# Attention, soft experts and a feed-forward in one kernel: other step order, alternating transposes, four feed-forward blocks, late weight parts, rows spread by DMA

## The chip, the cores and the metric

The kernel runs on one core of one Trainium2 chip. A core has TensorE (PE, with the weight loads PEld beside it), VectorE (DVE), ScalarE (ACT), GpSimd (POOL) and SyncE (SP), which here only issues transfers, and 16 DMA engines. The metric is the device time in microseconds.

## The reference

Three layers follow each other. All inputs are float32 but for the feed-forward's two weights, which the kernel reads as pairs of 32-bit words.

```python
# 1. attention: q, k, v are (4, 8, 576, 64)
q_d, k_d, v_d = means over groups of 4 positions          # 144 positions
out_up    = repeat(softmax(q_d k_d^T / 8) v_d, 4 times)
out_local = softmax(q k^T / 8 where |i - j| < 4) v
x = (out_up + out_local) as (2304, 512)
# 2. soft experts: phi (512, 32), w1 (8, 512, 1024), w2 (8, 1024, 512)
logits = x phi
slot_in = softmax(logits over tokens)^T x                  # 32 slots, 4 for each expert
slot_out[e] = relu(slot_in[e] w1[e]) w2[e]
y = softmax(logits over slots) slot_out                    # (2304, 512)
# 3. feed-forward: w_in (512, 2048), w_out (2048, 512)
out = relu(y w_in) ** 2 w_out
```

## The kernel before

**Attention.** A unit is two heads of one batch: 16 units, four for each batch. The work of a unit is cut into some thirty pieces, each with a letter, and a step `s` runs one piece of each letter for the unit `s - LAG[letter]`, in the order of a string (`ORDER`, or `ORDERS[s]` for single steps). 19 steps are issued in this order exactly: every engine's queue gets its instructions in program order and works through them in order. The letters that matter here:

- `Q`, `L`: SP loads q and k two units ahead, and v. `l`, `o`: SP loads weights, as many as `LOADN` and `LOADO` say for the step.
- `K`, `T` (`transposes`): PE transposes k or q, head by head, ACT (and DVE for one part of four) copies the result from PSUM. PSUM's general buffers `t` are three in turn.
- `d`, `b` (`downsample`): POOL sums q or k over groups of four.
- `M`, `S`: mask and local scores on PE. `R`: maximum and difference on DVE. `E`: exponential on ACT. `n`: sums on DVE. `P`: POOL multiplies. `p`: PE transposes the probabilities, DVE copies them.
- `s`, `m`, `e`, `N`, `q`: the same for the down-sampled attention (scores, maxima, three exponentials, sums and POOL's product pn, transposes).
- `V`, `v`, `w`, `D`: the value matmuls, their sums, and the down-sampled values; ACT writes xd. `A`: DVE adds both into xt.
- `t`: logits of xt; after the last unit of a batch also the gating statistics (`stage_g1`). `X`, `Y`: xt transposed into token rows. `g`, `G` (`stage_g2`, `stage_g3`): transposes and the matmul sip that gathers the slots' inputs, once for each batch.
- `F`, `H`, `J`: matmuls without use, as many as `FN` says, to keep PE at work. `c`: narrowing steps, as `CONV` says.

**Weights.** Every weight comes in pieces of 512 KB (w1 32, w2 32, w_in 16, w_out 16) in the fixed order of the list `loads`; `LPOS` says where w_in's pieces stand in it. `load_next` issues the next piece if a buffer is free: 32 of the ring, four of the pool `wa`, two and six more when attention's buffers are given up. w_in and w_out have to be narrowed from pairs of words to one float32: five operations a piece (`narrow`), on DVE, the first on ACT after the experts. `NORDER` is the order of narrowing, and `NEXP`, `NSTEPS` and `ACHAIN` say how many of these operations are issued at each place.

**Experts.** For each of eight: `expert_up` (the slots times w1, PE), `expert_mid`, `expert_down` (w2).

**Feed-forward.** As y is a product of the gates and 32 slots, `slots_in(j)` multiplies the slots by a quarter j of w_in (tile ap, 32 matmuls) and `slots_rows(j)` spreads the result over the partitions by four matmuls with a selection matrix (tile arp); ACT and DVE write the parts into `ast`. `ffn_up(c, f)` makes a 128 x 384 piece of the hidden layer from `ast` and the gates, ACT and DVE square it and split it into ghi and glo (for the pairs in `BYV` DVE takes the square for glo), and `ffn_down(c, f)` multiplies both by the split piece f of w_out: nine matmuls of 512 columns. Steps (c, f) run over six token blocks c and 16 pieces f, in blocks of f that `FB` gives; `ffn_up` is two steps ahead. At the end of a block, `partial` copies the sums out of PSUM (first block) or adds them to what is kept (DVE, later blocks). `SPLIT` says at which step a piece of w_out is split, `SLOTS` at which step `slots_in` (i) and `slots_rows` (r) of a quarter stand; quarter 0 and quarter 1's `slots_in` are in `ACHAIN`, the list of work between the experts and the first step.

Of the kernel before, what the change touches and what calls it, by code (L numbers as in the profile page):

```python
# [22 lines left out]
NE = 8  # L23
# [15 lines left out]
CONV = {19: 3}  # L39
# [4 lines left out]
LOADN = {0: 3, 1: 2, 2: 2, 3: 2, 4: 0, 5: 1, 6: 3, 7: 3, 8: 2, 9: 3, 10: 2, 11: 4, 12: 4, 13: 4, 14: 3, 15: 3, 16: 4, 17: 3, 18: 3, 19: 3}  # L44
LOADO = {0: 1, 1: 2, 2: 1, 3: 1, 4: 1, 5: 1, 6: 1, 7: 0, 8: 0, 9: 0, 10: 2, 11: 1, 12: 2, 13: 0, 14: 0, 15: 4, 16: 2, 17: 4, 18: 3, 19: 4}
# [3 lines left out]
ORDERS = {0: 'dSqvNRKsogPleMTnHXDFAcYwEmLtbpGJQV', 1: 'dYqSREVHvnocsJLPlKwmgFAeNTDtbpGMXQ', 2: 'dYSVHREvqnlwgPKcsmGoDAeTbMNptJLQFX', 3: 'dYHSVRvEqnwlgPGKsmDFAeTNJLtpMXcoQb', 15: 'dYSVHREvqnlwgPKcsmoGDeTANtbpJLQXFM', 16: 'dYSqREVHvwngPlKoGsmDFAceJLNtbpMXQT', 17: 'dYsqVHvJLGTwgRPNloMSDFAEncetbpmXQK', 18: 'dYSVHREvqnlgPwKcmGoDAseTNtbpJLQFXM'}  # L49
FN = {'F': [0, 3, 1, 0, 0, 0, 0, 0, 0, 0, 0, 0, 0, 0, 0, 4, 1, 10, 0, 0], 'H': [6, 1, 0, 0, 0, 0, 0, 0, 0, 0, 0, 0, 0, 0, 0, 1, 0, 2, 0, 0], 'J': [1, 4, 1, 0, 0, 0, 0, 0, 0, 0, 0, 0, 0, 0, 0, 0, 9, 0, 1, 0]}  # L50
LATE = 16
LOADS = 'Q0 L0 phi Q1 L1'
START = 22
DDVE = ()
DCOPY = ((1, 0, 1),)
PCOPY = (0, 4, 5)
CHAIN = (5, 0, 4)
# [7 lines left out]
NEXP = {(3, 0): 1, (3, 1): 1, (3, 2): 1, (3, 3): 1, (4, 0): 1, (4, 1): 1, (4, 2): 1, (4, 3): 1, (5, 0): 1, (5, 1): 1, (5, 2): 1, (5, 3): 1, (6, 0): 1, (6, 1): 1, (6, 2): 1, (6, 3): 1}  # L65
WRES = 0
ACHAIN = 'S1 T f1 g2 g3 g4 n4 f2 a0 f2 r0 r1 a1 W0 n2 n1 u0 u1 f3 n1 f3'
NSTEPS = (3, 1, 2, 2, 2, 2, 2, 2, 2, 3, 1, 2, 2, 1, 0, 2, 1, 2, 2, 2, 2, 2, 1, 0, 1, 0, 1, 0, 3, 1, 1, 0, 1, 2, 0, 1, 1, 1, 2, 0, 0, 3, 1, 0, 0, 2, 1, 0, 1, 0, 1, 1, 0, 2, 1, 0, 0, 1, 3, 1, 0, 0, 1, 3)
NSTEP = 1
FB = (0, 8, 12, 16)  # L70
SPLIT = {2: 1, 4: 2, 6: 3, 8: 4, 10: 5, 12: 6, 14: 7, 26: 8, 28: 9, 36: 10, 41: 11, 50: 12, 58: 13, 65: 14, 73: 15}
# [1092 lines left out]
```

## Time and profile before

| | |
|---|---|
| time, median of 3 | 455.02 us (454.85 to 456.29) |
| profiled execution | 454.35 us, span 452.7 us |
| mean granted clock of PE | 0.97 |
| PE busy | 415.7 us, 92% of the span |
| DVE, ACT, POOL busy | 293.1, 270.3, 96.5 us |
| bytes moved by DMA | 70.54 MB |

The span runs from the first to the last instruction; the time holds the start and end of the execution too. PE's busy time counts matmuls from start to end, so it also holds matmuls that are pipelined. Attention lies before about 165 us of the profile, the experts from 173 to 218 us, and the feed-forward behind them.

### The profile page before, as it was taken

Reading aid. Unit: us, or ns where it says so; the run is one execution under the profiler, and the core shown is the slowest. Engines: PE = TensorE matmul, PEld = TensorE weight load, DVE = VectorE, ACT = ScalarE, POOL = GpSimd, SP = SyncE. Lnnn points to the kernel's source line nnn. Section 1 sums busy time; section 2 is a strip of 40 time slices with the busy share of each in tenths; the row PEclk is TensorE's granted clock in tenths of the full one; section 3 lists DMA queues with packets and bytes.
Section 4 is the critical chain, followed back from the end, with each engine's and each line's share of the span. In section 5 each row is a group of like instructions: output and inputs, shape, how many; then the busy total and the mean of one; then the engine's idle time right before and its main releaser. Section 6 shows DMA issues by size and latency. Waiting matters only on the chain.

```text
span 452.7 us, 11645 instructions
## 1 busy us (share of the span) xinstructions
PE 415.7 (92%) x4548; PEld 319.2 (71%) x4548; DVE 293.1 (65%) x693; ACT 270.3 (60%) x670; POOL 96.5 (21%) x178
## 2 busy tenths in 40 slices
PE   7898899889988879987979999999999999999996
PEld 5576667657757745542568888888888888888885
DVE  3466647765775541398599899877935646576564
ACT  3478657866766521213388987688757656544551
POOL 8555645546654500030000000000000000000000
PEclk8899989998998998996999999999999999999999
DMA  7999999999331382999998000000000000012113
GB/s 180 373 327 277 265 301 270 267 265 252 99 98 24 107 276 103 363 409 409 409 408 319 1 0 1 1 2 0 0 1 0 1 1 2 0 38 103 70 71 139
DMA packets 43248, 70.54 MB, mean 156 GB/s; under 512 B 24378, under 2 KB 24634, under 8 KB 43194
## 3 DMA queue, kind: packets, MB, share of 16 engines
q1 hardware_dynamic: 43050, 69.68, 47.1%
q8 instruction: 36, 0.59, 0.5%
q14 instruction: 18, 0.15, 0.1%
q10 hardware_dynamic: 144, 0.13, 0.1%
HBM read 65.07 MB, written 4.72 MB: 154 GB/s over the span
## 4 chain that ended last, share of the span: by engine, by line
PE 73%; DVE 9%; ACT 9%; DMA 4%; issue 2%; POOL 1%; ACTq 0%; DVEq 0%; POOLq 0%; SPq 0%
PE po L1095 43%; DMA w<-in_moe_w_dram 4%; PE up L1015 4%; PE s L446 3%; PE hp L877 3%; DVE xt L588 2%; PE so L906 2%; PE ptp L519 2%; PE xp L623 2%; ACT kz L411 2%; PE lgt L604 1%; DVE elp L458 1%; PE av L562 1%; DVE mx L457 1%; ACT xd L580 1%
## 5 line engine op out<-in xcount | busy, mean ns | idle before, releaser
L1095 PE MATMUL po<-wparts,ghi 128*128 128x512 f32 x576 | 148.4, 392 | 1.8 <-ACT ghi L1023 1.3
L1095 PEld LDWEIGHTS po<-wparts,ghi 128*128 128x128 f32 x576 | 106.9, 188 | 22.7 <-ACT ghi L1023 1.5
L1095 PE MATMUL po<-wparts,glo 128*128 128x512 f32 x288 | 81.5, 390 | 0.5 <-DVE glo L1028 0.5
L1020 ACT ACTIVATE r<-up 128x384 f32<-128x384 f32 x96 | 47.2, 492 | 55.0 <-PE up L1015 46.1
L1028 DVE TENSOR_TENSOR glo<-r,ghi 128x384 fp32r<-128x384 f32 x94 | 52.4, 557 | 35.6 <-ACT ghi L1027 31.5
L1095 PEld LDWEIGHTS po<-wparts,glo 128*128 128x128 f32 x288 | 54.0, 188 | 12.1 <-DVE glo L1028 0.9
L1024 DVE TENSOR_TENSOR r<-r 128x384 f32<-128x384 f32 x44 | 24.4, 555 | 22.2 <-ACT ghi L1023 22.1
L1015 PE MATMUL up<-cst,ast 128*128 128x384 f32 x96 | 32.9, 344 | 0.0
L500 POOL TENSOR_TENSOR pl<-elp,sm 64x350 f32<-64x350 f32 x32 | 24.7, 772 | 26.5 <-PE tr L406 20.7
L415 ACT ACTIVATE qt<-tr 64x320 f32<-64x320 f32 x64 | 28.0, 438 | 1.1
L1026 ACT ACTIVATE r<-r 128x384 f32<-128x384 f32 x50 | 26.2, 525 | 1.6
L1027 ACT CAST ghi<-r 128x384 fp32r<-128x384 f32 x50 | 25.7, 514 | 1.6
L1023 ACT ACTIVATE ghi<-r 128x384 fp32r<-128x384 f32 x46 | 24.1, 525 | 1.5
L463 ACT ACTIVATE elp<-elp 128x350 f32<-128x350 f32 x16 | 7.9, 495 | 27.2 <-DVE elp L458 27.2
L411 ACT COPY kz<-tr 64x320 f32<-64x320 f32 (+1 forms) x48 | 20.6, 429 | 3.0 <-PE tr L406 1.3
L509 POOL TENSOR_TENSOR pn<-pd,sm 128x435 f32<-128x435 f32 x16 | 14.7, 917 | 33.0 <-DVE sm L508 33.0
L428 POOL TENSOR_TENSOR s<-kz 64x288 f32<-64x288 f32 x32 | 21.2, 663 | 1.3
L1015 PEld LDWEIGHTS up<-cst,ast 128*128 128x128 f32 x96 | 18.0, 188 | 4.1 <-issue 0.6
L877 PE MATMUL hp<-w,sT 128*32 128x256 f32 x256 | 18.3, 418 | 2.4 <-DMA w<-in_moe_w_dram 1.9
L457 DVE TENSOR_REDUCE mx<-s 128x10 f32<-128x350 f32 x16 | 8.3, 518 | 18.4 <-PE s L446 18.4
L906 PE MATMUL so<-w,ht 128*32 128x256 f32 x256 | 17.6, 406 | 1.2 <-DMA w<-in_moe_w_dram 0.5
L562 PE MATMUL av<-pt,vw 64*64 64x73 f32 x640 | 14.9, 234 | 3.5 <-DVE pt L520 3.5
(205 smaller groups left out, 710.4 us busy)
## 6 DMA issues: line engine op xcount, KB each, us to landing
w<-in_moe_w_dram SPq DMA_DIRECT2D x64, 512.0 KB, 8.2
win<-in_moe_w_in_dram SPq DMA_DIRECT2D x16, 512.0 KB, 10.1
wout<-in_moe_w_out_dram SPq DMA_DIRECT2D x16, 512.0 KB, 10.9
vw<-in_v_dram SPq DMA_DIRECT2D x62, 80.0 KB, 6.2
q<-in_q_dram SPq DMA_DIRECT2D x16, 288.0 KB, 4.4
k<-in_k_dram SPq DMA_DIRECT2D x16, 288.0 KB, 4.5
out_dram<-o SPq DMA_DIRECT2D x17, 256.0 KB, 2.1
vw<-in_v_dram SPq DMA_DIRECT2D x2, 64.0 KB, 2.5
```

Of the source, the lines that this page charges most:

```text
L411: (nc.vector.tensor_copy if (j, h, r) in DCOPY else nc.scalar.copy)(out=o, in_=i_)
L415: nc.scalar.mul(out=o, in_=i_, mul=1.0 / 128.0)
L500: nc.gpsimd.tensor_tensor(out=pl[r, :, c0:c0 + W], in0=el[r], in1=sm[r, 0:NB].unsqueeze(2).to_broadcast([64, NB, W]), op=ALU.mult,)
L877: nc.tensor.matmul(t[32 * g:32 * g + 32], sT[:, kt], got["w1", e, kt][:, 256 * g:256 * g + 256], start=(kt == 0), stop=(kt == 3), tile_pos ...
L906: nc.tensor.matmul(so[32 * g:32 * g + 32], ht[:, g // 2, j], got["w2", e, j][:, g // 2, 256 * (g % 2):256 * (g % 2) + 256], start=(e == 0 ...
L1015: nc.tensor.matmul(t, ast[:, 128 * f:128 * f + 128], cst[:, c * n:c * n + n], start=True, stop=True)
L1020: nc.scalar.activation(out=r, in_=t, func=AF.Relu)
L1024: nc.vector.tensor_tensor(out=g, in0=r, in1=r, op=ALU.mult)
L1026: nc.scalar.activation(out=g, in_=r, func=AF.Square)
L1027: nc.scalar.copy(out=ghi, in_=g)
L1028: nc.vector.tensor_tensor(out=glo, in0=g, in1=ghi, op=ALU.subtract)
L1095: nc.tensor.matmul(po[c][i], a[:, 128 * i:128 * i + 128], w[f], start=(first and w is whi and a is ghi), stop=(last and a is glo), skip_gr ...
```

## The change

- **Start.** An exponential of two numbers is ACT's first instruction. The local mask is made ahead of the other constants. DVE clears kz instead of POOL. `START`, the matmuls without use ahead of step 0, goes from 22 to 24.
- **Transposes.** The five transposes of each of two heads alternate, in two PSUM buffers, instead of one head after the other.
- **Order of a step.** `ORDER` and eight `ORDERS` are new, with `LOADN`, `LOADO`, `CONV`, `FN` and `CHAIN`. In the common step, `p` now stands ahead of `t`, `M` and `b` ahead of `N` and `X`, `P` behind `D`, `d` behind `n`, `g` behind `S` and `G` ahead of `K`.
- **Loads.** w_in's first quarter stands at place 43 of `loads`; the other three come behind all experts, between w_out's pieces (`TAIL`), all into the ring. They are issued only while more than 2 + `parts` ring buffers are free, and the rest of the list goes on in the feed-forward, after each step. `parts` starts at 9, the buffers that `partial` will need.
- **Narrowing.** `NORDER`, `NEXP`, `NSTEPS`, `SPLIT` and `BYV` are new; in the experts eight narrowing calls instead of 16, all in experts 5 and 6.
- **Feed-forward.** Four blocks of four f instead of 8, 4 and 4. Quarters 1 to 3 of w_in have their `slots_in` at steps 16, 40 and 60. Behind it SP issues 16 transfers of 32 rows that spread the result into `selq` (`slots_copies`), and at steps 18, 44 and 70 `slots_split` writes `ast` from there. `slots_rows` is left for quarter 0 alone.

```diff
-ORDER = 'HYdSVREvqnlwgPKcsmoGDeTAFNtbpLJXQM'
+ORDER = 'YFSgREVLvqwndGKHJsmDPeTAoptQMbNXcl'
-CONV = {19: 3}
+CONV = {10: 1, 12: 1, 15: 3, 18: 1, 19: 2}
-FN = {'F': [0, 3, 1, 0, ..., 4, 1, 10, 0, 0], 'H': [6, 1, 0, ...], 'J': [1, 4, 1, 0, ..., 0, 9, 0, 1, 0]}
+FN = {'F': [0, 1, 1, 0, ..., 4, 0, 10, 0, 0], 'H': [10, 5, 2, ...], 'J': [1, 4, 3, 0, ..., 0, 7, 3, 0, 0]}
-START = 22
+START = 24
-CHAIN = (5, 0, 4)
+CHAIN = (5, 4, 4)
-LPOS = [30, 30, 30, 30, 42, 42, 42, 42, 72, 72, 72, 72, 76, 76, 76, 76]
-SLOTS = {2: ['r1'], 29: ['i2'], 33: ['r2'], 62: ['i3'], 64: ['r3']}
-NORDER = 'w,w w,w w,w w,w o0 o1 o2 o3 o4 o5 o6 o7 w,w o8 o9 w,w o10,o11 w,w w,w o12,o13 o14,o15'
-ACHAIN = 'S1 T f1 g2 g3 g4 n4 f2 a0 f2 r0 r1 a1 W0 n2 n1 u0 u1 f3 n1 f3'
-FB = (0, 8, 12, 16)
+LPOS = [43, 43, 43, 43]
+TAIL = 'o0 o1 i1 o2 o3 o4 o5 o6 o7 i2 o8 o9 o10 o11 i3 o12 o13 o14 o15'
+SLOTS = {16: ['i1'], 18: ['r1'], 40: ['i2'], 44: ['r2'], 60: ['i3'], 70: ['r3']}
+NORDER = 'w,w w,w o0 o1 o2 o3 w,w o4 w,w o5 o6 o7 o8 w o9 w,w o10 w o11 o12 w,w o13,w w o14 o15'
+ACHAIN = 'S1 T n1 f1 g4 g2 g3 a0 f2 n4 f1 r0 r1 W0 f2 n2 n1 f2 u0 f3 n1 u1 f3'
+FB = (0, 4, 8, 12, 16)
...
+    first = cp.tile([1, 2], F32, name="first")
+    nc.scalar.activation(out=first, in_=ones2, func=AF.Exp)
...
-            if any(j > 1 and (j, i // 2) not in win for k, i, j in got if k == "win") and kind != "win":
-                if sum(x[0] is ring for x in free) < 2:
-                    fits = [x for x in fits if x[0] is not ring]
+            if kind == "wout" or kind == "win" and j > 0:
+                if sum(x[0] is ring for x in free) <= 2 + parts[0]:
+                    return
...
-            nc.gpsimd.memset(t, 0.0)
+            nc.vector.memset(t, 0.0)
             kzs.append(t)
...
-                for h in range(2):
-                    t = bt([128, 5, 64], f"tr{u}_{j}{h}")
-                    hr = slice(64 * h, 64 * h + 64)
-                    for i in range(5):
-                        m = min(128, 9 * D - 128 * i)
-                        nc.tensor.transpose(t[0:m, i], st[nm][hr, 128 * i:128 * i + m], ident[hr, hr])
+                ts = [bt([128, 5, 64], f"tr{u}_{j}{h}") for h in range(2)]
+                for i in range(5):
+                    m = min(128, 9 * D - 128 * i)
+                    for h, t in enumerate(ts):
+                        hr = slice(64 * h, 64 * h + 64)
+                        nc.tensor.transpose(t[0:m, i], st[nm][hr, 128 * i:128 * i + m], ident[hr, hr])
...
+    def slots_copies(j):
+        raws[j] = selq
+        for g in range(4):
+            for x in range(4):
+                nc.sync.dma_start(out=raws[j][32 * x:32 * x + 32, g], in_=asb[j][32 * g:32 * g + 32])
+    def slots_split(j):
+        t = raws.pop(j).rearrange("p g c -> p (g c)")
+        a = ast[:, 512 * j:512 * j + 512]
+        nc.scalar.copy(out=a, in_=t)
+        nc.vector.tensor_tensor(out=a[64:128], in0=t[64:128], in1=a[64:128], op=ALU.subtract)
...
                 slots_in(j, up(f"ap{j}", [128, 128]))
+                slots_copies(j)
             else:
-                slots_rows(j, up(f"arp{j}", [128, 512]), range(4))
+                slots_split(j)
...
         ffn_down(*steps[i - LOOK])
+        load_next(len(loads))
```

## Rows read from the trace of the kernel before

**Rows 1.** Busy us by stretch: PE, PEld, DVE, ACT, POOL; clock, DMA share, GB/s.
```profile
102.00:104.00 2.00, 2.00 (x31) 1.48 (x33) 0.74 (x2) 1.01 (x3) 1.78 (x4) 0.50 0.89 263
200.00:210.00 10.00, 6.91 (x91) 2.80 (x91) 9.43 (x25) 3.16 (x14) 0.94 (x1) 0.84 1.03 408
237.40:291.00 53.60, 53.60 (x251) 44.49 (x254) 48.77 (x97) 44.75 (x88) 0.00 (x0) 1.00 0.18 70
291.00:345.00 54.00, 54.00 (x274) 45.19 (x263) 37.39 (x72) 40.59 (x80) 0.00 (x0) 1.00 0.00 1
```

**Rows 2.** Timeline, a plain attention step; start, us, engine, line, operation.
```profile
80.63 0.47 PE L604 MATMUL lgt<-xt,phis 128*32 128x128 f32 x16 [0.85 <-DVE xt L588]
...
80.68 1.83 ACT L415 ACTIVATE qt<-tr 64x320 f32<-64x320 f32 x4
...
82.56 0.64 PEld L446 LDWEIGHTS s<-kz,qt 128*29 128x29 f32 x40 [0.32 <-ACT qt L415]
```

**Rows 3.** Timeline, the step after a fourth unit.
```profile
90.66 0.82 PE L446 MATMUL s<-kz,qt 128*29 128x70 f32 x40
...
99.08 0.41 ACT L580 ACTIVATE xd<-av 128x288 f32<-128x288 f32 x1 [2.34 <-PE av L575]
...
103.37 1.24 PE L446 MATMUL s<-kz,qt 128*29 128x70 f32 x40
```

**Rows 4.** Chain that ended last, experts; start, us, what.
```profile
191.40 1.86 PE so L906 x32
...
195.49 1.30 PE so L906 x21
...
217.20 0.68 PE so L906 x8
```

**Rows 5.** Timeline, the start of the feed-forward.
```profile
219.96 1.29 DVE L227 SCALAR_TENSOR_TENSOR win<-win,win 128x512 int32<-128x512 int32 x2
...
228.76 1.65 PE L1095 MATMUL po<-wparts,ghi 128*128 128x512 f32 x6 [1.28 <-ACT ghi L1023]
```

**Rows 6.** Chain that ended last, the feed-forward's even part.
```profile
237.38 2.06 PE po L1095 x9
...
288.75 2.06 PE po L1095 x9
...
292.19 2.06 PE po L1095 x9
...
300.94 0.89 PE arp L1002 x8
```

**Rows 7.** Timeline, the first attention step.
```profile
6.29 1.28 ACT L411 ACT_TABLE_LOAD   x1 [6.29 <-PE tr L406]
...
9.12 1.67 PE L357 MATMUL lgt<-warmb 128*128 128x256 bf16 x7
```

**Rows 8.** Timeline of SP's queue: first issues, and first and last expert loads.
```profile
1.72 0.33 SPq L384 DMA_DIRECT2D vw<-in_v_dram  x1
...
2.09 2.70 SPq L393 DMA_DIRECT2D vw<-in_v_dram  x4
...
176.78 0.81 SPq L168 DMA_DIRECT2D w<-in_moe_w_dram  x2
...
198.03 9.28 SPq L168 DMA_DIRECT2D w<-in_moe_w_dram  x8
```

**Rows 9.** DMA issues: KB each, median us to landing.
```profile
w<-in_moe_w_dram SPq DMA_DIRECT2D x64, 512.0 KB, 8.2
...
out_dram<-o SPq DMA_DIRECT2D x17, 256.0 KB, 2.1
```

**Rows 10.** Groups of DVE instructions, 225 to 453 us: busy us, mean ns, idle before.
```profile
L1028 DVE TENSOR_TENSOR glo<-r,ghi 128x384 fp32r<-128x384 f32 x94 | 52.4, 557 | 35.6 <-ACT ghi L1027 31.5 <-PE po L1095 0.7
...
L1079 DVE TENSOR_TENSOR part<-po,part 128x512 f32<-128x512 f32 x18 | 11.3, 682 | 0.0
...
L227 DVE SCALAR_TENSOR_TENSOR w<-wout,w 128x512 int32<-128x512 int32 x16 | 10.7, 686 | 0.1
```

More of the change, by code (lines that the diff above doesn't have):

```diff
@@ L138, in attention_moe_ffn_kernel @@
     got, where = {}, {}
+    parts = [9]
     free = deque((ring, f"r{i}") for i in range(NRING))
@@ L142, in attention_moe_ffn_kernel @@
         loads += [("w1", e + 1, j) for j in range(4) if e + 1 < NE] + [("w2", e, j) for j in range(4)]
-    loads += [("wout", f, 0) for f in range(FF // 128)]
-    wins = [("win", i, j) for j in range(4) for i in range(4)]
-    for x, at in sorted(zip(wins, LPOS), key=lambda y: -y[1]):
-        loads.insert(at, x)
+    for i, at in sorted(enumerate(LPOS), key=lambda y: (-y[1], -y[0])):
+        loads.insert(at, ("win", i, 0))
+    for x in TAIL.split():
+        j = int(x[1:])
+        loads += [("wout", j, 0)] if x[0] == "o" else [("win", i, j) for i in range(4)]
     loads = deque(loads)
@@ L178, in load_next @@
             fits.sort(key=lambda x: x[0] is not wa)
-            if kind == "wout" or kind == "win" and (LPOS[4 * j + i] > 50 or lb is None) or kind != "win" and i == NE - 1:
+            if kind == "wout" or kind == "win" and (j > 0 or LPOS[i] > 50 or lb is None) or kind != "win" and i == NE - 1:
                 fits = [x for x in free if x[0] is ring]
@@ L200, in attention_moe_ffn_kernel @@
     free.extend((wa, f"w{i}") for i in range(4))
-    maskf = wa.tile([128, 1024], F32, tag="w0", name="maskf")[:, 0:W]
-    nc.gpsimd.memset(maskf, 0.0)
-    for g in range(4):
-        m = maskf[32 * g:32 * g + 32]
-        nc.gpsimd.affine_select(out=m, in_=m, pattern=[[1, W]], compare_op=ALU.is_ge, fill=NEG, base=0, channel_multiplier=-1)
-        nc.gpsimd.affine_select(out=m, in_=m, pattern=[[-1, W]], compare_op=ALU.is_ge, fill=NEG, base=6, channel_multiplier=1)
-    maskb = cp.tile([128, NB, W], BF16, name="maskb")
-    nc.vector.tensor_copy(maskb, maskf.unsqueeze(1).to_broadcast([128, NB, W]))
-    nc.vector.memset(maskb[0:32, 0:2, 0:3], NEG)
-    nc.vector.memset(maskb[96:128, NB - 2:NB, W - 7:W], NEG)
     def narrow(dst, raw):
@@ L231, in narrow_win @@
         if (j, i // 2) not in win:
-            pool, tag = place = min((x for x in free if x[0] is (wa if j < 2 else ring)), key=lambda x: x[0] is wa and x[1])
+            pool, tag = place = min((x for x in free if x[0] is (wa if j < 1 else ring)), key=lambda x: x[0] is wa and x[1])
             free.remove(place)
+            where["w32", j, i // 2] = place
             win[j, i // 2] = pool.tile([128, 2, FF // 4], F32, tag=tag, name=f"win{j}_{i // 2}")
@@ L956, in attention_moe_ffn_kernel @@
     load_next(len(loads))
-    assert not loads, loads
     act_abs.append(1)
@@ L995, in slots_in @@
                 )
+        for i in range(2):
+            if where["w32", j, i][0] is ring:
+                done("w32", j, i)
         asb[j] = xq.tile([128, 128], F32, tag="asb", bufs=2, name=f"asb{j}")
@@ L1006, in slots_rows @@
         nc.vector.tensor_tensor(out=a[64:128, c], in0=t[64:128, c], in1=a[64:128, c], op=ALU.subtract)
+    raws = {}
+    def slots_copies(j):
+        raws[j] = selq
+        for g in range(4):
+            for x in range(4):
[5 more added lines that the diff above has]
+        nc.vector.tensor_tensor(out=a[64:128], in0=t[64:128], in1=a[64:128], op=ALU.subtract)
     NF, NC = FF // 128, B * S // TCH
@@ L1073, in partial @@
                     free.remove(place)
+                    parts[0] -= 1
                     pair = ring.tile([128, 2, DM], F32, tag=place[1], name=f"part{c}_{i}")
@@ L1133, in attention_moe_ffn_kernel @@
         ffn_down(*steps[i - LOOK])
+        load_next(len(loads))
+    assert not loads, loads
 _INS = ['q', 'k', 'v', 'moe_phi', 'moe_w1', 'moe_w2', 'moe2_w_in', 'moe2_w_out']
```

32 lines of the change are left out of this document (21 added, 11 removed).

## Prediction

> **What bounds the kernel now.** I read the table by stretches first, then the chain that ended last, then the timeline of single steps. The stretches show three regimes [rows 1]. In attention PE's granted clock is 0.50 in places, as from 102 to 104 us. From 200 to 210 us, in the experts, the DMA moves 408 GB/s and PE is busy for 6.9 of 10 us. From 237 us on PE is busy without a gap and the clock is 1.00; DVE is at 48.8 of 53.6 us, so it is the second limit there.
>
> A plain attention step lasts 8.10 us, from one score block to the next (82.56 to 90.66 us) [rows 2, 3]. The score block was released by ACT's copies of q (80.68 to 82.51), not by PE, which had waited 0.85 us for xt earlier [rows 2]. ACT goes from copy to copy the whole step, so a plain step is ACT's queue plus the scores and the maximum behind them. In the step after every fourth unit the distance is 12.71 us (90.66 to 103.37) [rows 3]: the gating matmuls sip stand on PE ahead of the values, ACT waits 2.34 us for these, and PE then runs at a granted clock of 0.50 [rows 1, 3], its lower level, 1.2 GHz; the scores take 1.24 instead of 0.82 us. PE had stood idle in pieces before that.
>
> In the experts the chain is PE up to 196.8 us, with 4.09 us from one expert's second product to the next, and then DMA until 217.2 us [rows 4]. A load of 512 KB takes 1.28 us at 408 GB/s. The feed-forward then needs until 228.76 us for its first product and until 237.38 us for its even pace, 2.234 us a step (237.38 to 288.75 us are 23 steps) [rows 5, 6].
>
> **The change part by part.** The sum is made against the profiled execution: 454.35 us, a span of 452.7 us and 1.65 us around it. The median of the runs is 0.67 us above it; I add that at the end.
>
> *Start.* ACT loads its activation table (1.28 us) at its first copy, while the transposed k waits [rows 7]. An early exponential takes this off. But two more warming matmuls precede k's transposes and eleven instead of seven the first scores, 0.24 us each [rows 7]. I take it that 0.4 us of the 1.28 are lost again: -0.9. Bounds: -1.3 (all kept) and +0.2 (all six matmuls on the path). The masks come earlier and DVE clears kz in place of POOL; both lie beside the wait for k. Were that cover gone, they would cost what POOL's clearing cost, some 1 us; the range of the start holds that nearly.
>
> *Transposes of two heads in turn.* They use different partitions and banks, so they may overlap. But ACT's copies of k are behind other copies on ACT, and those of q behind the exponentials. So I take nothing. The second head's bank is freed by an ACT copy, so the first transposes may start 0.1 to 0.2 us later: up to +2 over some ten plain steps.
>
> *Order of a plain step.* The transposes of the probabilities move ahead of the logits, into PE's 0.85 us wait for xt, and free about 0.7 us behind xt. But ACT's q copies end at the same instant and still release the scores [rows 2]. POOL does k's sums before the normalisation pn, whose reader on PE comes some 3 us later. SP's issues change places by a few instructions, and q, k and v are there a step ahead. Zero, -1 to +2 over all plain steps.
>
> *Order of the gating step, three times.* The gating transposes and their two ACT copies move ahead of the exponential, where ACT waits for DVE. DVE copies the probabilities before the maximum of the logits, so the value matmuls start earlier. sip now comes ahead of k's transposes: k's copies on ACT start only after sip, but scores_down and the values run beside them on PE. Laid out with the durations of this step, xd comes 0.9 us earlier than 99.08, and PE's part behind it is 0.7 to 1.2 us shorter, so the scores start near 101.9 instead of 103.37: -1.45 each, -4.4 together. Bounds: -1.8 each, and 0 if k's copies behind sip cost what the rest gives.
>
> *w_in's later parts.* Before, 28 loads lie between the first issue after attention (176.78 us) and the last expert weight: 24 of w1 and w2 and four of w_in's second quarter; the third and fourth quarter already come behind (first and last issue in [rows 8]). The 44 buffers are full at the end of attention either way, and the first quarter must still be there. So it is not twelve loads that leave the front but four: 4 x 1.28 = -5.1 us. PE's floor is 195.49 + 3 x 4.09 + 1.86 us for the last product [rows 4] + an estimated 1.5 us for the gate copies between = 211.1 against 217.9 us: no more than -6.8. If only half of the four come off the path: -2.5.
>
> *Start of the feed-forward.* DVE's narrowing of w_out's first piece waits for its load in both. Behind it now stand three double operations of w_in's first quarter (at most 1.29 us each [rows 5]), so ap starts about 2 us later after the last expert. In return the second quarter's operations, its ap and its arp leave this stretch, and the pieces of w_out follow directly. Added up along DVE and ACT, the first product comes 10.4 us after the experts (10.9 before: 217.88 to 228.76 us) and the third, from which the pace is even, after 15.4 (17.3 before, 237.38 - 2.23 - 217.88): -1.9; -3 to +1.
>
> *Rows by DMA.* ap costs PE 1.21 us (288.75 to 292.19 is 3.44 us instead of 2.23), arp 0.9 [rows 6]. Before, two of each lie in the even part; after, three ap and no arp: -0.6. Each part now needs 16 copies of 16 KB by SP. No row shows one. Nearest below: a single small load, issued 0.37 us ahead of the next, and the 2.1 us that an output takes to land; above: 0.67 us an issue (four in 2.70) and an estimated 2.5 us [rows 8, 9]. So 16 x 0.37 + 2.1 = 8.0 us, up to 13.2; I take the lower, since that load has nearly the same size, 15 KB. ACT wants the first part two steps (4.5 us) later and PE looks two steps ahead, of which ACT's and DVE's own work leaves 2.1 us: slack 6.6 us. Stall 1.5 us (0 to 6.6). The second part has four steps, slack 11.1: 0, at most 2; the third has ten. Behind the waiting copy on ACT stand the squares, and PE's next products wait for these.
>
> A weight load takes 8.2 us to land [rows 9], yet SP issues eight in 9.28 us [rows 8], so loads overlap. The Trainium skill (DMA: Bandwidth & Descriptors, Rules for kernel authors) says to coalesce small transfers, as below 64 KB one pays mostly overhead; with its fixed 2.0 us for each copy in a row, the first part would take an estimated 32 us and stall ACT for 25. The trace's overlapping loads disagree with adding it up.
>
> *Four blocks.* The matmuls stay the same. In the 24 steps from the third on DVE has 48.8 us before [rows 1]. The change adds four partial copies (4 x 0.68), three quarters of a narrowed piece (four operations of at most 0.69 us: 2.1), three squares as long as a glo (3 x 0.56) and one row part (as long as a copy, 0.7) [rows 10]: 56.0 us against 53.6 + 1.2 us of PE. So DVE is full there, and PE waits when DVE lags more than its look-ahead, about 2 us: +1.5 (0 to +5, with the third block as full). The 18 additions of the two middle blocks (12.3 us) fall where DVE was at 37.4 of 54 us or less [rows 1].
>
> Sum: -0.9 + 0 - 4.4 - 5.1 - 1.9 - 0.6 + 1.5 + 1.5 = -9.9: 444.45 us for such an execution, 445 for the median.
>
> **Rivals.**
> *Attention gives nothing* (k's copies behind sip; start at +0.2): 450 us. For it: ACT's queue sets the plain steps and is not shortened. Against: the waits that are reordered are in the rows.
> *Everything falls in place*: experts at PE's floor, no stall in the feed-forward, gating steps at -1.8: 437 to 441 us. For it: PE's clock has much to give back in attention.
> *DVE bounds the feed-forward*: +5 instead of +1.5 and nothing gained at its start: 450.5 us. For it: the count above; against: the last block and the end are light.
> *The late loads change nothing* (buffers, not the queue, hold the experts): -5.1 falls away: 450 us.
> *The other side: copies behind loads.* If weight loads are in SP's queue ahead of the row copies, each adds 1.28 us to the first and the second part. With n of them the stalls are 1.5 + 1.28 n and 1.28 n - 3.1 us. From five on the gain is gone (455 us), with eight it is 462. For it: 28 loads are left at the end of the experts. Against: they need 36 us, and the sixteenth step comes some 46 us behind the experts; later loads come only as narrowing frees buffers, one in about 5 us. The Trainium skill (the same page, Queues, rings and completion order) says that what SP issues goes on one row of rings whose descriptors are consumed in order: by that rule this case follows wherever a load is under way.
>
> **How the numbers follow.** Likeliest, 442 to 448 us: 0.42. All in place: 0.18. One of the cases with part of the gain (448 to 453.6 us): 0.27. Within 0.3%, about what a measurement of this kernel can tell from no change (453.7 to 456.4): 0.05. Slower: 0.08. So faster 0.87. The bounds added up give 437 to over 460 us; leaving out one in ten on each side gives 439 to 452.5.
>
> **What would show it.** Right: no table load behind k's transposes; score blocks 8.1 us apart, near 11.3 in gating steps; the last expert some 40 us after its first product began; the feed-forward's steps at 2.234 us with 3.44 at three places, and an ACT wait for a DMA near the eighteenth. Wrong: gating steps still at 12.7; PE waits for glo in the first 24 steps; an ACT wait beyond 8 us for the rows; plain steps other than 8.1 us.

## The result and the profile after

The changed kernel takes 448.5 us (median of four runs, 447.92 to 449.58) where the kernel before takes 455.65 (454.85 to 456.37) beside it: 0.985 of the time, 95% interval 0.982 to 0.988. The forecast was 445.0 us with a range of 439 to 452.5: the sign and the range hold, and 7.2 us came of the 10 forecast. The profiled execution took 449.58 us, the longest of the four and 4.8 less than that of before; the sum had 9.9. In all ratios here executions in a slower state of the chip are left out, so a ratio need not be the quotient of the two medians.

That 4.8 is the difference of two large numbers. Attention and the experts became 11.6 us shorter (the first expert product starts at 165.51 us for 172.77 before, and the last one at 205.56 for 217.20 [rows 4]), and the feed-forward became 6.8 us longer (from the start of that last product to the last product of `ffn_up`: 225.1 us before, 231.9 after). The timeline of PE has these products, first before, then after:
```profile
172.77 3.50 PE L877 MATMUL hp<-w,sT 128*32 128x256 f32 x32 [0.38 <-DVE sT L827]
...
442.30 0.34 PE L1015 MATMUL up<-cst,ast 128*128 128x384 f32 x1
```
```profile
165.51 2.79 PE L883 MATMUL hp<-w,sT 128*32 128x256 f32 x24 [0.38 <-DVE sT L833]
...
205.56 0.64 PE L912 MATMUL so<-w,ht 128*32 128x256 f32 x8
...
437.50 0.34 PE L1039 MATMUL up<-cst,ast 128*128 128x384 f32 x1
```
The other rows, in the order of the stages:

The timeline of ACT in the first step (start, us, engine, line, operation, idle time before and what ended it), against [rows 7]:
```profile
0.80 1.28 ACT L113 ACT_TABLE_LOAD   x1 [0.80 <-PEq L1176]
...
5.75 1.31 ACT L417 COPY kz<-tr 64x320 f32<-64x320 f32 x3 [3.45 <-PE tr L410]
```
The table is loaded 5.5 us earlier, and the copy of k now waits for PE's transposes alone. The first scores start at 9.08 us; before, at 10.76.

The timeline of a gating step, against [rows 3]:
```profile
87.58 0.81 PE L452 MATMUL s<-kz,qt 128*29 128x70 f32 x40 [0.54 <-ACT qt L421]
...
94.98 0.41 ACT L586 ACTIVATE xd<-av 128x288 f32<-128x288 f32 x1
...
98.23 0.81 PE L452 MATMUL s<-kz,qt 128*29 128x70 f32 x40 [0.53 <-ACT qt L421]
```
xd comes 7.40 us after the scores (8.42 before), ACT doesn't wait for it any more, the scores are 10.65 us apart (12.71 before), and PE is at its upper clock at the end of the step (0.81 us for a score block, where [rows 3] has 1.24).

One step that was plain before is not so any more. The timeline of PE in it:
```profile
70.30 0.33 PE L543 MATMUL vdp<-ident,vt 128*75 128x128 f32 x1
72.30 0.37 PE L543 MATMUL vdp<-ident,vt 128*75 128x128 f32 x1 [1.67 <-issue]
```
PE stood for 1.67 us between two transposes of one value block, for nothing that the profile shows ("issue"), and after it the clock fell. The step took 11.53 us in place of 8.10.

The chain that ended last, from the experts into the feed-forward, against [rows 4, 5]:
```profile
195.70 0.92 PE hp L883 x16
196.64 10.15 DMA wout<-in_moe_w_out_dram
206.92 0.43 DVE w L226
...
210.67 0.43 PE ap L997 x8
```
The experts' end still waits for transfers, as PE's table of waits from 160 to 222 us has it (us in total, times, longest), and right behind these transfers stands w_out's first piece:
```profile
PE so L912 <- DMA w<-in_moe_w_dram: 1.8, 3, 0.6
```
The first product of `ffn_down` starts at 216.17 us, 9.9 us after the experts (10.9 before).

And the place where the time went back. A step of the feed-forward is counted here from the start of its `ffn_up` product to the start of the next one, so what `SLOTS` puts at step 16 lengthens step 15. The timeline of SP, PE and ACT from the first product of a late part on:
```profile
249.68 10.30 SPq L1024 DMA_DIRECT2D selq<-asb  x16
...
261.40 0.62 ACT L1030 CAST ast<-selq 128x512 fp32r<-128x512 f32 x1 [6.76 <-DMA selq<-asb]
261.93 0.48 ACT L1044 ACTIVATE r<-up 128x384 f32<-128x384 f32 x1
...
262.46 0.44 PE L1039 MATMUL up<-cst,ast 128*128 128x384 f32 x1 [4.00 <-ACT r L1044]
```
The page's DMA issues (count, KB each, median us to landing) have the same copies, and the table of waits of ACT (us in total, times, longest), from 240 to 340 us, has two of the three splits:
```profile
selq<-asb SPq DMA_DIRECT2D x48, 16.0 KB, 1.8
```
```profile
ACT ast L1030 <- DMA selq<-asb: 9.6, 2, 6.8
```
The sixteen issues stand one behind another on SP, 0.64 us apart; the last copy lands 11.7 us after the first was issued. ACT asks for the result in the eighteenth step, waits 6.76 us, and behind this wait stands the relu that frees the bank of PE's next product: PE waits 4.00 us and comes out of it at the lower clock. Busy time from 263 to 270 us (PE, PEld, DVE, ACT, POOL; clock, DMA share, GB/s):
```profile
263.00:270.00 7.00, 6.98 (x24) 5.64 (x25) 6.66 (x14) 5.69 (x12) 0.00 (x0) 0.76 0.26 103
```
Steps 19 and 20 take 6.40 and 4.31 us in place of 2.235: 6.25 us lost, 4.00 of them standing and 2.25 at the lower clock. The second part's split waits 2.8 us, and steps 46, 48 and 51 lose 2.4 us more.

### The profile page after: what moved, and what is told of

Its sections match the earlier page's. It is cut to its first block, busy times and chain, and to the rows that moved or that the text cites. A ratio compares the mean times of both kernels' runs of the same rounds, so it can differ in the third digit from the quotient of the medians.

```text
span 447.9 us, 11703 instructions
## 1 busy us (share of the span) xinstructions
PE 412.7 (92%) x4550; PEld 312.2 (70%) x4550; DVE 298.5 (67%) x712; ACT 269.9 (60%) x671; POOL 94.9 (21%) x177
## 4 chain that ended last, share of the span: by engine, by line
PE 55%; DVE 4%; DMA 3%; SPq 2%; issue 1%; ACT 1%; DVEq 0%; ACTq 0%
PE po L1120 42%; PE hp L883 4%; PE up L1039 3%; PE so L912 3%; DMA wout<-in_moe_w_out_dram 2%; SPq L1024 2%; PE ap L997 1%; PE lgt L362 1%; DVE win L231 1%; PE stp L831 0%; DVE part L1104 0%; DVE glo L1052 0%; DMA selq<-asb 0%; DVE w L231 0%; PE ctp L719 0%
## 5 line engine op out<-in xcount | busy, mean ns | idle before, releaser
L1120 PE MATMUL po<-wparts,ghi 128*128 128x512 f32 x576 | 150.0, 395 | 0.6 <-ACT ghi L1047 0.5
L1120 PE MATMUL po<-wparts,glo 128*128 128x512 f32 x288 | 82.7, 394 | 1.7 <-DVE glo L1052 1.6
L1048 DVE TENSOR_TENSOR r<-r 128x384 f32<-128x384 f32 x48 | 26.6, 554 | 18.0 <-ACT ghi L1047 17.9
L1047 ACT ACTIVATE ghi<-r 128x384 fp32r<-128x384 f32 x50 | 26.3, 525 | 1.6
L1050 ACT ACTIVATE r<-r 128x384 f32<-128x384 f32 x46 | 24.2, 526 | 1.5
L1051 ACT CAST ghi<-r 128x384 fp32r<-128x384 f32 x46 | 23.6, 514 | 1.4
L1104 DVE TENSOR_TENSOR part<-po,part 128x512 f32<-128x512 f32 x36 | 22.5, 680 | 0.0
L452 PE MATMUL s<-kz,qt 128*29 128x70 f32 x640 | 13.0, 225 | 7.1 <-ACT qt L421 7.1
L912 PE MATMUL so<-w,ht 128*32 128x256 f32 x256 | 16.7, 384 | 2.2 <-DMA w<-in_moe_w_dram 1.8
```

Source lines behind the costliest of these rows:

```text
L912: nc.tensor.matmul(so[32 * g:32 * g + 32], ht[:, g // 2, j], got["w2", e, j][:, g // 2, 256 * (g % 2):256 * (g % 2) + 256], start=(e == 0 ...
L1047: nc.scalar.activation(out=ghi, in_=r, func=AF.Square)
L1048: nc.vector.tensor_tensor(out=g, in0=r, in1=r, op=ALU.mult)
L1050: nc.scalar.activation(out=g, in_=r, func=AF.Square)
L1051: nc.scalar.copy(out=ghi, in_=g)
L1120: nc.tensor.matmul(po[c][i], a[:, 128 * i:128 * i + 128], w[f], start=(first and w is whi and a is ghi), stop=(last and a is glo), skip_gr ...
```

## The experiments

Each kernel ran beside the kernel before on one chip; the four runs 1 to 4, 5 to 8 and 9 to 12 share a chip. The medians of before there are 455.37, 455.15 and 455.44 us, so the chips differ by some tenths. The medians are over all executions of a run. "First expert" and "last expert" are the start of the experts' first and last products in the profiled execution.

| run | us (median) | of before (95%) | first expert | last expert |
|---|---|---|---|---|
| the changed kernel | 448.5 | 0.985 (0.982 to 0.988) | 165.5 | 205.6 |
| 1 first product earlier | 442.1 | 0.970 (0.962 to 0.978) | 167.5 | 207.8 |
| 2 rows by TensorE | 442.1 | 0.970 (0.961 to 0.980) | 165.2 | 202.8 |
| 3 second quarter early | 454.6 | 0.996 (0.992 to 1.001) | 168.4 | 215.0 |
| 4 old attention order | 455.1 | 0.999 (0.995 to 1.002) | 170.5 | 209.7 |
| 5 both products earlier | 446.3 | 0.977 (0.971 to 0.984) | 168.9 | 207.7 |
| 6 one head after the other | 451.2 | 0.992 (0.987 to 0.997) | - | - |
| 7 before, early Exp | 455.1 | 0.998 (0.994 to 1.002) | 170.6 | 215.7 |
| 8 run 5, fewer loads | 446.7 | 0.981 (0.974 to 0.988) | 165.2 | 206.6 |
| 9 splits later | 444.5 | 0.978 (0.973 to 0.982) | 163.7 | 205.7 |
| 10 run 9, fewer loads | 443.4 | 0.975 (0.971 to 0.980) | 162.4 | 203.3 |
| 11 run 9, no early Exp | 443.7 | 0.974 (0.969 to 0.979) | 167.0 | 207.3 |
| 12 run 9, head after head | 445.2 | 0.980 (0.975 to 0.984) | 170.5 | 209.2 |

Leaving out two executions far off the rest, in runs 6 and 7, the executions of one kernel in this table spread by 3 to 8 us (those of the changed kernel by 1.7), so differences under some 2 us between two rows are read in the traces, not here.

**Run 1: the first product of a late part earlier.**
```
-SLOTS = {16: ['i1'], 18: ['r1'], ...
+SLOTS = {14: ['i1'], 18: ['r1'], ...
```


> The changed kernel (448.5 us) with one edit: the product of the first late slot part (and with it its 16 row copies) is asked for two steps earlier, at step 14 in place of 16; its split stays at step 18. Theory A: the 6.25 us that steps 19 and 20 lost are the 16 copy issues, one behind another on SP at 0.62 us each, overrunning the two steps of slack. Two more steps are 4.47 us more slack, so about 1.8 us of the stall stay and the time is about 444.1 us. Rival B: the stall is a backlog of VectorE and ScalarE (quarter 1's narrowing and the partial sums), which the earlier product only moves forward by two steps: 448.5 to 450 us, with the loss now at steps 15 to 18.

442.1 us. The wait on ACT did what theory A says. Its timeline:
```profile
247.13 10.32 SPq L1024 DMA_DIRECT2D selq<-asb  x16
258.87 0.62 ACT L1030 CAST ast<-selq 128x512 fp32r<-128x512 f32 x1 [2.30 <-DMA selq<-asb]
```
The copies take as long as before (10.32 us), the wait has gone from 6.76 to 2.30 us, that is by the two steps, and PE sees next to nothing of the rest: steps 19 and 20 take 2.24 and 2.45 us. So 6.0 of the 6.25 us came back and not 4.5: two more steps are more than the 4.00 us that PE stood, and without the standing the lower clock behind it is gone too. Nothing is lost at steps 15 to 18, which rules out rival B. Steps 46 and 48 are as long as in the changed kernel.

**Run 2: the rows by TensorE.**
```
             if x[0] == "i":
                 slots_in(j, up(f"ap{j}", [128, 128]))
-                slots_copies(j)
             else:
-                slots_split(j)
+                slots_rows(j, up(f"arp{j}", [128, 512]), range(4))
```


> The changed kernel with one edit: the rows of parts 1 to 3 are spread by TensorE (four selection products, as in the kernel before) and not by 48 DMA copies. Theory A (the copies' issue time is what steps 19 and 20 wait for): the 6.25 us go, and three products of about 0.9 us come back on TensorE, so about 445.0 us (448.5 - 6.25 + 2.7). Rival B (backlog of VectorE and ScalarE): the loss stays and the products come on top, about 451 us.

442.1 us, 3 less than theory A. The three products cost what was expected (3.05 us steps at three places, 0.8 each), but the second block's 2.4 us went with the first block's loss, all but 0.2 us at step 51: steps 46 and 48 take 2.24 us, and the table of PE's waits from 230 to 425 us is empty, with the same four blocks, the same narrowing and the same sums on DVE. So what I had put down to DVE at the end of the second block needs the row copies too.

**Run 3: w_in's second quarter back ahead of the last experts' weights.**
```
-LPOS = [43, 43, 43, 43]
-TAIL = 'o0 o1 i1 o2 ...
+LPOS = [43, 43, 43, 43, 43, 43, 43, 43]
+TAIL = 'o0 o1 o2 ...
...
-            if kind == "wout" or kind == "win" and j > 0:
+            if kind == "wout" or kind == "win" and j > 1:
```
The second quarter then no longer waits for free ring buffers, as in the kernel before.

> The changed kernel with one edit: the second quarter of w_in (four pieces of 512 KB) is loaded right behind the first quarter, ahead of the last experts' weights, as in the kernel before; it is narrowed where it was. Theory A: the experts' end waits for the weight transfers, and the 4.4 us that the experts became shorter are these four pieces going behind: the last product of the experts ends 4 to 5 us later, and the time is about 453 us. Rival B: the experts became shorter for another reason (the earlier end of attention left more time for transfers, or fewer narrowing steps lay between), and the time stays at 448.5 us.

454.6 us, 6 more. Its chain that ended last, where the changed kernel's has one wait of 10.15 us for w_out:
```profile
192.24 10.48 DMA w<-in_moe_w_dram
202.79 10.16 DMA w<-in_moe_w_dram
212.99 1.08 PE so L912 x8
```
Two waits of 10 us for the experts' own weights stand in a row. From the first product to the start of the last it is 46.6 us; in the changed kernel 40.1. Theory A holds, and the four pieces cost 6.6 us here, more than the 5.1 of four transfers at 408 GB/s. This execution took 458.96 us, 4.4 above the run's median; by the two profiles 2.8 us of its distance from the changed kernel lie ahead of the experts, 6.6 in them and nothing behind.

**Run 4: the old order of attention.** The edit puts ORDER, ORDERS, FN, START, CHAIN, PCOPY, CONV, LOADN and LOADO back.


> The changed kernel with the attention order of the kernel before: its step orders, warm-up counts, its loads and narrowing per step and its choice of copy engine; the two heads' turns in the transposes, the early Exp, the late w_in and the four blocks stay. Theory A: the order gave the gating steps' 2.1 us each and 0.4 us behind each (7.5 us), less the odd step's 3.4 us, plus some of the first two intervals' 2.6 us: the experts begin 4 to 6.5 us later and the time is 453 to 455 us. Rival B: the experts' end is set by the transfers alone, which begin no later, and absorb a later start: 448.5 to 450 us. Rival C: the order itself is worth nothing and the transposes in turn or the early Exp carried it: 448.5 us with gating steps of 10.5 us.

455.1 us, 6.6 more, at the upper end of theory A. The gating steps are 11.60, 11.69 and 11.69 us, and no step between them is longer than 8.23 us; PE's halt stands elsewhere in this run (1.63 us at 44.8 us). The first expert starts 5.0 us later and the last one 4.1 us later: rival B's absorption is 0.9 us at most, as the second and fourth expert alone are 2.0 us shorter here, without the lower clock and the halt that they have in the changed kernel. The gating steps are not the 12.7 of [rows 3] either. Busy time by stretch, the second gating step, in this run and before:
```profile
91.28:102.97 11.69, 9.68 (x176) 6.47 (x176) 7.75 (x22) 7.40 (x26) 5.28 (x9) 1.00 0.98 282
```
```profile
90.66:103.37 12.71, 10.55 (x175) 7.37 (x175) 7.75 (x22) 7.63 (x26) 6.23 (x10) 0.90 0.91 258
```
At the full clock the order is worth 1.1 us a step, and the rest of the 2.1 in the pair of profiles is the stretch at 0.50 [rows 1]. No gating step of the new order fell into it in any profile here but the disturbed one of run 6 (10.47 to 10.79 us); of the old order's steps in run 7 one did.

**Run 5: both products earlier.**
```
-SLOTS = {16: ['i1'], 18: ['r1'], 40: ['i2'], ...
+SLOTS = {14: ['i1'], 18: ['r1'], 38: ['i2'], ...
```


> The changed kernel with the products of the first and the second late slot part both two steps earlier (14 for 16, 38 for 40). Theory A (the second block's loss at steps 46, 48 and 51, 2.4 us, is the same cause: the second part's 16 copies end after its split is asked for, ScalarE waits, VectorE's half of the split and its three partial sums come late, and glo with them; the run with the rows on TensorE has no loss there): both losses go, 448.5 - 6.25 - 2.4 = 439.9 us, steps 46, 48 and 51 at 2.24 us. Rival B (VectorE is overfull at the end of the second block, and the run on TensorE only shifted it): 442.1 us as with the first part alone, steps 46 and 48 still long.

446.3 us, worse than run 1: both theories missed it. Steps 46 and 48 did fall (0.8 us lost in place of 2.4), but steps 37 and 38 take 6.55 and 3.89 us. The timeline there, PE and DVE:
```profile
300.79 0.86 PE L997 MATMUL ap<-win,soT 128*32 128x128 f32 x24
301.05 0.42 DVE L230 TENSOR_SCALAR win<-win 128x512 int32<-128x512 int32 x1
301.50 0.69 DVE L231 SCALAR_TENSOR_TENSOR win<-win,win 128x512 int32<-128x512 int32 x1
302.11 1.88 DVE L1104 TENSOR_TENSOR part<-po,part 128x512 f32<-128x512 f32 x3
303.91 0.68 DVE L232 SCALAR_TENSOR_TENSOR win<-win,win 128x512 int32<-128x512 int32 x1
304.64 0.43 PE L997 MATMUL ap<-win,soT 128*32 128x128 f32 x8 [3.00 <-DVE win L232]
```
The product of part 2 needs w_in's third quarter, whose last narrowing operation is now asked for as PE stands there, and three partial sums lie in between. Asking earlier for the product asked earlier for its operand.

**Run 6: transposes one head after the other.**
```
-                for i in range(5):
-                    m = min(128, 9 * D - 128 * i)
-                    for h, t in enumerate(ts):
-                        ...
+                for h in range(2):
+                    t = bt([128, 5, 64], f"tr{u}_{j}{h}")
+                    for i in range(5):
+                        ...
```


> The changed kernel with one edit: the ten transposes of a part run one head after the other again, not in turn. The prediction has this part at nothing. Theory A: nothing, 448.5 us, gating steps of 10.5 us. Rival B: the run with the old order but heads in turn had gating steps of 11.6 us where the kernel before has 12.7, so about 1.1 us of a gating step come from the turns (copies of the first head start earlier or later): three times 1.1 and perhaps the first steps, 451.5 to 453 us.

451.2 us (446.84 to 452.74 but for one disturbed execution of 1313.7 us, which was the profiled one, so its intervals are not read). Between the theories; run 12 settles it.

**Run 7: the early Exp alone, in the kernel before.**
```
+    first = cp.tile([1, 2], F32, name="first")
+    nc.scalar.activation(out=first, in_=ones2, func=AF.Exp)
```
Its input `ones2`, there already, is made ahead of it.

> The kernel before (455.4 us) with one edit: an Exp on two elements at the start, so that the table is loaded ahead of k's first copies. Theory A (the start's gain of 1.7 us is the 1.3 us table load and nothing else): first scores at 9.4 us where they were at 10.8, time about 454 us. Rival B: the start is set by something else (the mask's making, the identity), first scores at 10.8 us, 455.4 us.

The table load went to 0.80 us and the first scores came at 9.87 us (10.76), but the time is that of before. In its profile PE stands for "issue" twice near 36 and 42 us, by 1.07 and 0.98 us; even so the first expert starts 2.2 us and the last one 1.5 us earlier than before [rows 4]. That is lost behind the experts: PE's granted clock is 0.56 from 216 to 222 us (1.00 before, from 218 to 222), and the first product of `ffn_down` starts at 229.45 us, 0.7 later than in [rows 5]. What the edit is worth at the end of the kernel stays open. Two gating steps take 11.61 and 11.67 us here, at a clock of 1.00, and one 12.84, at 0.89.

**Run 8: fewer weight loads in steps 5 to 8 of attention, in run 5's kernel.**
```
-LOADN = {..., 5: 3, 6: 4, 7: 3, 8: 3, ...
+LOADN = {..., 5: 1, 6: 1, 7: 1, 8: 1, ...
```


> The kernel of the run with both products early, and in steps 5 to 8 of attention only one weight piece is asked for behind q and k in each step (3, 4, 3 and 3 before). Theory A: TensorE's halt between two vdp products in the eighth interval is its own instruction stream arriving late (the halt ended 1.4 to 1.6 us after a 16 KB transfer of the instruction queue in each of five runs), because that transfer shares the DMA engines with weight loads at 100% busy: with the engines less busy the halt shrinks below 0.5 us and the seventh and eighth intervals are 8.1 to 8.5 us; the time is 437 to 438 us, unless the pieces put off make the experts longer by as much. Rival B: the halt is the fetch's own latency at that place of the program and does not mind the loads: intervals as before, 440 us or more.

The halt is gone: the seventh and eighth intervals are 8.09 us each (11.53 in the changed kernel, 12.73 in run 5 for the eighth). Busy time by stretch of the changed kernel (PE, PEld, DVE, ACT, POOL; clock, DMA share, GB/s):
```profile
60.00:68.00 8.00, 7.28 (x167) 5.54 (x163) 5.51 (x16) 6.21 (x20) 4.96 (x8) 1.00 1.07 331
68.00:76.00 8.00, 6.32 (x132) 4.85 (x132) 3.45 (x10) 3.17 (x9) 4.28 (x8) 0.76 0.99 270
```
and of run 8:
```profile
60.00:68.00 8.00, 7.24 (x167) 5.64 (x163) 5.24 (x16) 6.22 (x20) 4.52 (x8) 1.00 0.66 206
68.00:76.00 8.00, 7.28 (x167) 5.56 (x163) 5.42 (x17) 6.20 (x20) 5.17 (x9) 1.00 0.65 184
```
With the DMA at two thirds PE does not stand and keeps its clock there. But the time did not fall (446.7 for 446.3): the first expert starts 3.7 us earlier than in run 5, the last one only 1.1 us earlier. Theory A's reservation, that the pieces put off make the experts longer, is not what the traces show: in both runs 44 pieces are issued before the first expert and 21 of the experts' follow it, and PE waits 2.3 us for them here and 2.4 in run 5. The second expert, in run 8 and in run 5:
```profile
168.58:173.87 5.29, 5.07 (x101) 2.85 (x97) 1.51 (x6) 1.15 (x4) 0.00 (x0) 0.82 0.50 142
```
```profile
172.08:176.44 4.36, 4.14 (x101) 2.47 (x97) 1.51 (x6) 1.15 (x4) 0.00 (x0) 1.00 0.52 160
```
The lower clock takes 0.9 us here, and a halt of 0.91 us in the fourth expert makes that one 1.2 us longer; the rest is 0.2 us each in the first expert and at the end.

**Run 9: the splits later, the products where they were.**
```
-SLOTS = {16: ['i1'], 18: ['r1'], 40: ['i2'], 44: ['r2'], ...
+SLOTS = {16: ['i1'], 22: ['r1'], 40: ['i2'], 47: ['r2'], ...
```


> The changed kernel with one edit: the first and second late parts' splits, which wait for the row copies, are asked for at steps 22 and 47 in place of 18 and 44, ahead of their first use at steps 24 and 48; the products and copies stay. The copies then have six and seven steps of 2.24 us (13.4 and 15.6 us) for 16 issues of 0.62 us and a landing of 1.8 us (11.7 us together). Theory A: both losses of the feed-forward go (6.25 and 2.4 us): 448.5 - 8.65 = 439.9 us, every step 2.24 us but the three with a product. Rival B: a split so close to its first use makes the product wait for ScalarE's and VectorE's halves (0.6 and 0.7 us behind a backlog): steps 24 and 48 long by 1 to 3 us each, 442 to 445 us.

444.5 us. ACT waits for no copy any more, and steps 18 to 24 take 2.24 us: the 6.25 us are back, as in run 1, by another edit. At the second part rival B is right. PE and DVE there:
```profile
320.09 1.87 DVE L1104 TENSOR_TENSOR part<-po,part 128x512 f32<-128x512 f32 x3
...
323.05 0.69 DVE L1031 TENSOR_TENSOR ast<-selq,ast 64x512 fp32r<-64x512 f32 x1
...
323.80 0.44 PE L1039 MATMUL up<-cst,ast 128*128 128x384 f32 x1 [1.85 <-DVE ast L1031]
```
The rows are there, but DVE's half of the split stands behind three partial sums and a glo, and the product that needs it waits 1.85 us: step 47 takes 4.26 us. Of the 2.4 us at this place some 0.3 came back.

**Run 10: run 9 with run 8's loads.**


> The kernel with late splits, and one weight piece in place of 3, 4, 3 and 3 behind q and k in steps 5 to 8 of attention. Theory A: the halt of TensorE in the eighth interval (2 to 4 us with what follows at the lower clock) is gone again, and the experts begin earlier by that, but their end is set by the transfers, which are not earlier: the time is within 1 us of the run with late splits. Rival B: the gain of the halt reaches the end: 2 to 3 us faster than the run with late splits.

443.4 us, 1.1 less, within the spread. Intervals 8.10 and 8.10; run 9's own halt was small in its profiled execution (8.09 and 8.55), so the pair adds little to run 8.

**Run 11: run 9 without the early Exp** (run 7's two lines taken out).


> The kernel with late splits, without the early Exp. Theory A: the table load of 1.3 us comes back behind k's first transposes, the first scores begin 0.9 to 1.3 us later, attention ends by as much later; since the experts' end waits for transfers, 0 to 1.3 us of it reach the end of the kernel. Rival B: the start gained from the mask being made first and the loads' order, not from the table: first scores at the same time.

The outcome of rival B, by another way. The first scores start at 9.03 us without the early Exp, as early as in any run with it (9.04 to 10.48). ACT's timeline:
```profile
2.73 1.28 ACT L415 ACT_TABLE_LOAD   x1 [2.73 <-DVE kz L328]
5.72 1.31 ACT L415 COPY kz<-tr 64x320 f32<-64x320 f32 x3 [1.70 <-PE tr L408]
```
The load stands ahead of ACT's first copy and waits for the clearing of kz, which the change gave to DVE; that comes early enough to load the table before k's transposes. In [rows 7] the load waited for PE's transposes. Either edit takes it off the path, and the second is worth nothing then. The first expert starts 3.3 us later than in run 9, but behind a halt of 2.03 us at 105.7 us, so this is not the table's.

**Run 12: run 9 with the transposes head after head.**


> The kernel with late splits, with the transposes one head after the other. Theory A: nothing, within 1 us of the run with late splits, and gating steps of 10.5 to 10.7 us. Rival B: the turns let both heads' copies start together and carry part of the gating steps: these become 11 to 11.6 us and the time 1 to 3 us longer.

Theory A: the gating steps are 10.55, 10.69 and 10.70 us, where run 9 has 10.47, 10.63 and 10.62, and the time is 445.2 for 444.5. The turns are worth 0.07 us a gating step. Its eighth interval is 13.65 us, with a halt of 2.95 us, so such a halt would be enough for run 6's loss; that it was the cause is not shown, as its own trace is of the disturbed execution.

## Why the prediction was right, and where it was off

The sign and the range hold, and so do the signs of the parts that were forecast with one. That the time lies in the range is in part luck: against the sum, 5.4 us came out better than forecast (start, early steps, gating steps) and 10.5 us worse (the halt, and the terms from w_in on). By the terms of the sum, from the profiled executions:

| term | forecast | measured |
|---|---|---|
| start, to the first scores | -0.9 | -1.7 |
| two early steps, other plain steps, end of attention | 0 | -2.7 |
| a halt of PE in one plain step | not in the sum | +3.4 |
| gating steps, three | -4.4 | -6.3 |
| w_in later | -5.1 | -4.4 |
| start of the feed-forward | -1.9 | -1.6 |
| products on PE | -0.6 | -0.5 |
| first part's rows | +1.5 | +6.3 |
| four blocks on DVE, second part's rows | +1.5 | +2.7 |

*Start.* The mechanism was right, the cause half: of two edits that each free the path of the table load (runs 7 and 11), I credited one and put the other, DVE's clearing of kz, down as hidden. The size lies within the spread of the runs, whose first scores start from 9.03 to 10.48 us.

*Early steps.* The first two steps were forecast at nothing and became 2.6 us shorter (7.31 and 8.27 us; 8.49 and 9.71 before). Busy time from 8 to 20 us, before, in run 7 and in the changed kernel:
```profile
8.00:20.00 12.00, 9.27 (x126) 5.96 (x130) 4.37 (x12) 7.17 (x21) 6.67 (x12) 0.82 0.98 324
```
```profile
8.00:20.00 12.00, 8.78 (x182) 5.97 (x179) 5.17 (x15) 6.46 (x20) 7.90 (x14) 1.00 0.96 316
```
```profile
8.00:20.00 12.00, 9.37 (x200) 6.62 (x202) 6.32 (x18) 6.77 (x20) 8.02 (x14) 1.00 0.95 328
```
The old order at the upper clock takes 7.91 and 8.54 us (run 7), so 1.7 us of the 2.6 go with the clock and 0.9 with the order and the rest of the change. Run 4, the old order at 0.58, takes 9.48 and 10.18. Which of the edits to order and warming keeps the clock up was not tried alone.

*Transposes in turn*: nothing, as predicted (run 12).

*Gating steps.* Forecast 1.45 us each, measured 2.1 against [rows 3] and 1.1 against run 4. The layout came out between: it used the durations of the step of before, with its stretch at the lower clock, as if they were the step's own.

*w_in later.* Run 3 shows the mechanism alone, at 6.6 us; 4.4 in the pair, forecast 5.1. The argument that only four of the twelve moved loads leave the front holds. The size was taken too low: from the seventh expert on the pair's experts are 6.0 us shorter, near the 6.8 that the prediction set as the most. The second and fourth expert took 1.5 us of it back, the second at a clock of 0.80 (1.00 before), the fourth with a halt of 0.47 us.

*Rows by DMA: the step that failed.* "I take the lower" of the two bounds for an issue, 0.37 us and 0.67 us [rows 8], because of its size in KB. Measured are 0.64 us, near the upper. With it the part's own formula gives 16 x 0.64 + 1.8 = 12.0 us (11.7 measured) against 6.6 of slack: 5.4 us, and 6.25 were lost. The near match hides two more errors. PE stood for only 4.00 us, so the slack was 7.7; and the 2.25 us at the lower clock behind the stall were not in the sum. Runs 1, 2 and 9 each took these 6.25 us back, or all but 0.2, by two steps more, by no copies, and by a later split. The small load of 0.37 us was a single one; the vw loads of 0.67, four in a row on the same queue, were the nearer row for a train of issues.

The rule of the Trainium skill that the prediction weighed (DMA: Bandwidth & Descriptors, Rules for kernel authors: coalesce small transfers) pointed the right way; by it, with a fixed 2.0 us that the page gives for transfers issued by GpSimd, I would have had an estimated 32 us for the part, and 11.7 us were measured. The trace agrees that small copies cost mostly overhead, 16 KB in 1.8 us, but the copies overlap and only their issue adds up.

*Four blocks.* DVE is less full than counted: in run 2, where nothing else stands, it is busy for 51.6 of 56.2 us in 24 steps (from 220.40 us on), where the count had 56.0. Alone it costs PE 0.3 us at step 14 and 0.2 at step 51. The 2.4 us at the second block's end need a split whose rows or whose DVE half come late beside the partial sums: without copies they are gone (run 2), with late splits DVE is the one waited for (run 9).

*Rivals.* The other side, weight loads in front of the row copies, did not come about: SP's queue has the sixteen copies without a load among them. "Attention gives nothing" and "the late loads change nothing" are ruled out by runs 4 and 3. Of the signs that were to show the prediction wrong one came, plain steps other than 8.1 us (the step with the halt, 11.53 us), and one nearly: an ACT wait for the rows of 6.8 us where 8 was set, with PE behind it. The other two, gating steps of 12.7 us and waits for glo in the first 24 steps, did not.

*What stays open.* The halts of PE (below) are in most of the traces here; where they can stand is known, but not why some of these places are hit and most are not. Runs 1 and 2 are the fastest measured, 442.1 us, and beat both kernels. A split of part 2 one or two steps earlier than in run 9 was not tried.

## What to carry to other kernels

A train of small DMAs costs its issue time on the queue, one behind another, and not its landing time: count issues times the interval between issues in the nearest train of the trace, and give the consumer that much slack in steps before it is asked to wait. The consumer's wait costs more than itself when the engine that waits also frees what the bound engine needs next, and the lower clock behind such a stall is to be counted too (here 2.25 us on 4.00); asking for it later, close to its use, did as much for the first part as asking for the source earlier, as long as neither lands behind a block of other work on the same engine. And a product that is moved forward takes its operand's preparation with it.

## What the hardware showed that was not expected

PE can stand for "issue" in the middle of a stretch of ready work. In ten of the thirteen traces read (all but those of the kernel before, run 9 and run 10) it stood so for 0.6 to 3.0 us at a time, and its next matmul came 1.2 to 1.7 us after the end of a 16 KB transfer of the queue that the page calls "instruction". The changed kernel's DMA queues from 69 to 71 us (packets, MB, share of 16 engines), just ahead of its halt at 70.6 to 72.3:
```profile
q1 hardware_dynamic: 393, 0.47, 103.2%
q8 instruction: 1, 0.02, 4.9%
```
36 such transfers bring 0.59 MB in the whole span, about one for each 256 of PE's 9205 instructions in the trace. The halts stand at these marks. In the twelve traces other than the one of before and the disturbed one of run 6, PE stood for "issue" 29 times by more than 0.13 us, and each time the number of its instructions that had started was 193 or 194 over a multiple of 256: 2497 or 2498 at the halt of the changed kernel and of runs 1, 2, 3, 5, 7, 9 and 12, 3778 in runs 5 and 11, 6082 in the fourth expert of run 8. The single one of before, 0.38 us, is not at such a mark. The clock falls after a halt (0.76 from 68 to 76 us), which makes 1.7 us of standing into 3.4 us of time. So the halts are instructions that come late. That busy DMA engines make them late is less sure: it fits runs 8 and 10, where the DMA was less busy in these steps and no halt was seen there (run 8 has one of 0.9 us later, in the experts), but the kernel before has none over 0.4 us with the engines as busy, and no run changes the instructions alone. The Trainium skill (Runtime: NRT & Kernel Launch, Instruction fetch mechanics) says that each engine's instructions are refilled in blocks of 16 KiB by a DMA queue of its sequencer, and that the cost is mostly hidden. The trace agrees on the size; here it was not always hidden.

A copy of 16 KB from SBUF to SBUF holds SP for 0.51 to 0.59 us and lands 1.7 to 1.9 us after its issue; in the changed kernel the trains of sixteen take 10.0 to 10.3 us in all three parts.
